# MLP biases as a broadcast second operand in two PSUM evacuations, with a new unit order

## The chip, the cores and the metric

One core of one Trainium2 chip. The time is the device time of one execution in microseconds (us); the kernel before takes 1090.31 us (median of 3 runs, 1090.11 to 1090.38). All runs quoted here are at a granted clock of 0.998 to 1.0. The same kernel spreads over more than that across rounds and chips: the kernel before had 9 runs from 1088.80 to 1092.16 us on one chip.

## The reference

An attention block whose output is gated by an MLP (S = 2048, D = 1024, 32 heads of 32, F = 3584):

```python
def _A_ref(x, wqkv, wo):                 # attention
    qkv = ...                            # x @ wqkv, split in heads
    scores = einsum("bhqd,bhkd->bhqk", q, k) * (Dh ** -0.5)
    o = einsum("bhqk,bhkd->bhqd", softmax(scores), v)
    return o.transpose(...) @ wo
def _B_ref(x, w1, b1, w2, b2):           # MLP
    h = gelu(layernorm(x) @ w1 + b1)     # tanh form of gelu
    return h @ w2 + b2
xn = layernorm(A_x)
return A_x + _A_ref(xn, ...) * silu(_B_ref(xn, ...))
```

## The kernel before

A planner in Python builds five instruction streams (one per engine) ahead of time. 512 attention units run one after the other; each takes one filler unit with it, in the order that the string PLAN gives: `a` = 1/28 of the first MLP matmul of a token chunk, `w2`..`w5` = one block of the second MLP matmul cut into 2 to 5 pieces, `q`, `v` = projections for the next heads, `o` = output projection, `.` = nothing. The loop, cut:

```python
while u < NU + LAG or ...:
    s_unit(u)                  # TensorE: scores, 32x128 tiles          (L872)
    fill_act(u)                # ScalarE: waiting tanh, if they fit     (L565, L609)
    exp_unit(u)                # ScalarE: two exponentials, 128x1024    (L884)
    ...                        # TensorE: one filler unit into bank 7   (L395)
    pv_unit(u - LAG)           # TensorE: P x V and row sums, 128x32    (L901, L904)
    run_dq(pg.clk["tensor"])   # VectorE: waiting gelu and softmax steps
```

The two evictions of the filler bank, and what follows the first of them (cut):

```python
x0 = op("vector", lambda e: e.tensor_scalar(xb[:, 0:n], bank(bk, 0, n), b1T[:, f:f + 1], None, op0=ALU.add),
   r=[("b", bk), "b1"], w=[kx], c=217 + 1.042 * n)                                   # L548
def square(): ... tensor_tensor(ub, xb, xb, mult)                                    # L554
def cube():   ... scalar_tensor_tensor(ub, ub, 1.0 / 0.044715, xb, add, mult)        # L558
def tanh():   ... activation(ut[:, :, 0:n], ut[:, :, 0:n], Tanh, scale=...)          # L565, ScalarE, two `a` at once
def gate():   ... scalar_tensor_tensor(hT, ut, 1.0, xq, add, mult)                   # L571
...
x0 = op("vector", lambda e: e.tensor_scalar(zh[:, 0:n], bank(bk, 0, n), 0.25, b2h[:, nb:nb + 1], op0=ALU.mult, op1=ALU.add),
   r=[("b", bk), "b2"], w=[kz], c=217 + 1.042 * n)                                   # L605
```

`c` is the planner's estimate of the duration in ns. It costs nothing on the chip, but the planner places the other VectorE and ScalarE operations by it. All filler units use bank 7, so the eviction of one filler has to be done before the next filler begins; in between lie the PV product and the next scores. `n` is 352 or 320 columns.

The softmax here doesn't subtract the row's maximum and nothing guards it: scores larger than these inputs give would overflow.

## Time and profile before

| | kernel before |
|---|---|
| time, us | 1090.31 |
| TensorE busy | 1078.1 us, 99% |
| ScalarE busy | 1043.9 us, 96% |
| VectorE busy | 627.6 us, 58% |
| L548, 352 / 320 columns | 584 / 551 ns |
| L605, 352 / 320 columns | 584 / 548 ns |
| score loads to filler loads | 0.33 us, with or without an eviction |

Two engines are nearly full and the third, which the change makes faster, is not. The lines behind this table are shown in the prediction, except the two of L605 (busy us, mean ns):

```profile
L605 DVE TENSOR_SCALAR zh<-ps,b2h 128x352 f32<-128x352 f32 x32 | 18.7, 584 | 141.6 <-PE ps L395 141.6
...
L605 DVE TENSOR_SCALAR zh<-ps,b2h 128x320 f32<-128x320 f32 x16 | 8.8, 548 | 41.8 <-PE ps L395 41.8
```

What is to be read from this profile is where TensorE can lose time at a unit boundary: in front of the scores, where it may wait for an exponential (L872 behind L884), and in front of the filler, where it may wait for the eviction (L395 behind L548 or L605).

### The profile page before, as it was taken

The page shows a single profiled execution, that of the slowest core. Times are in us where ns is not written, and L with a number is a line of the kernel's source. Part 1 is how long each engine was busy: PE and PEld are TensorE (multiplying, and loading weights), DVE is VectorE, ACT ScalarE, POOL GpSimd, SP SyncE. Part 2 cuts the span into 40 slices and gives each one's busy share as a digit, 9 for nine tenths or more (in the row PEclk, how much of TensorE's full clock was granted, in tenths as well). Part 3 has the DMA queues.
Part 4 walks back from the last instruction along what each step waited for, and adds up shares of the span by engine and source line. Part 5 has one row for each costly group of instructions (what it writes and reads, how often), then busy time and mean ns, then how long its engine had stood idle before and what let it go on. Part 6 is the DMA issues. An engine that isn't in the chain of part 4 may idle for free.

```text
span 1088.8 us, 61842 instructions
## 1 busy us (share of the span) xinstructions
PE 1078.1 (99%) x29167; PEld 701.4 (64%) x29167; DVE 627.6 (58%) x1396; ACT 1043.9 (96%) x1197; POOL 22.4 (2%) x69
## 2 busy tenths in 40 slices
PE   9999999999999999999999999999999999999998
PEld 6766666666666666666666666666666666666665
DVE  8487843477732576642377743378733387635556
ACT  7899998999999999999999999999999999999993
POOL 4400000000000000000000000000000000000000
PEclk9999999999999999999999999999999999999999
DMA  7944365413464214355333274423253343684534
GB/s 242 185 127 139 119 177 138 125 52 110 119 154 123 68 59 128 101 104 148 90 100 100 73 155 124 120 81 109 81 135 115 91 123 106 192 206 105 109 92 123
DMA packets 209336, 131.92 MB, mean 121 GB/s; under 512 B 52538, under 2 KB 200250, under 8 KB 209082
## 3 DMA queue, kind: packets, MB, share of 16 engines
q1 hardware_dynamic: 209082, 127.97, 43.4%
q8 instruction: 228, 3.74, 1.5%
q14 instruction: 26, 0.21, 0.1%
HBM read 104.87 MB, written 12.06 MB: 107 GB/s over the span
## 4 chain that ended last, share of the span: by engine, by line
PE 57%; ACT 41%; DVE 1%; DMA 0%; issue 0%; POOL 0%; SPq 0%
ACT P L884 37%; PE ps L395 34%; PE ps L872 9%; PE ps L901 6%; PE ps L904 6%; ACT u L565 4%; PE ps L705 1%; PE ps L689 1%; DVE stats L324 0%; DMA OT<-in_A_x_dram 0%; ACT thz L609 0%; DVE wq L669 0%; DVE hT L359 0%; ACT hT L716 0%; DVE wq L671 0%
## 5 line engine op out<-in xcount | busy, mean ns | idle before, releaser
L884 ACT ACTIVATE P<-ps 128x1024 bf16<-128x1024 f32 x1024 | 968.9, 1084 | 10.3 <-PE ps L872 5.4
L901 PE MATMUL ps<-P,VP 128*32 128x256 bf16 x4096 | 257.0, 273 | 0.5 <-issue 0.5
L904 PE MATMUL ps<-P,ones 128*32 128x256 bf16 x4096 | 256.8, 273 | 0.0
L395 PE MATMUL ps<-hT,war 128*32 128x352 bf16 (+1 forms) x5376 | 225.8, 309 | 0.1
L395 PE MATMUL ps<-yTc,war 128*32 128x352 bf16 (+1 forms) x5376 | 225.3, 309 | 0.0
L872 PE MATMUL ps<-QT,KT 32*128 32x256 bf16 x4096 | 203.7, 273 | 3.4 <-issue 0.6
L395 PEld LDWEIGHTS ps<-hT,war 128*32 128x32 bf16 x5376 | 128.0, 96 | 74.4 <-issue 25.8
L395 PEld LDWEIGHTS ps<-yTc,war 128*32 128x32 bf16 x5376 | 127.3, 96 | 74.2 <-DVE xb L548 18.9
L872 PEld LDWEIGHTS ps<-QT,KT 32*128 32x128 bf16 x4096 | 60.8, 92 | 115.6 <-issue 61.9
L605 DVE TENSOR_SCALAR zh<-ps,b2h 128x352 f32<-128x352 f32 (+1 forms) x48 | 27.5, 572 | 183.4 <-PE ps L395 183.4
L548 DVE TENSOR_SCALAR xb<-ps,b1T 128x352 f32<-128x352 f32 (+1 forms) x168 | 96.2, 573 | 48.7 <-PE ps L395 44.2
L571 DVE SCALAR_TENSOR_TENSOR hT<-u,xb 128x352 bf16<-128x352 f32 (+1 forms) x168 | 84.4, 509 | 68.3 <-ACT u L565 68.2
L901 PEld LDWEIGHTS ps<-P,VP 128*32 128x32 bf16 x4096 | 109.8, 97 | 21.3 <-issue 2.1
L904 PEld LDWEIGHTS ps<-P,ones 128*32 128x32 bf16 x4096 | 109.7, 97 | 18.6
L395 PE MATMUL ps<-xnT,wq 128*32 128x352 bf16 (+1 forms) x2688 | 112.7, 309 | 0.0
L395 PEld LDWEIGHTS ps<-xnT,wq 128*32 128x32 bf16 x2688 | 63.7, 96 | 37.2 <-DVE xb L548 8.9
L558 DVE SCALAR_TENSOR_TENSOR u<-u,xb 128x352 f32<-128x352 f32 (+1 forms) x168 | 82.5, 509 | 1.9
L554 DVE TENSOR_TENSOR u<-xb 128x352 f32<-128x352 f32 (+1 forms) x168 | 82.5, 507 | 0.7
L565 ACT ACTIVATE u<-u 128x704 f32<-128x704 f32 (+1 forms) x84 | 71.8, 859 | 0.0
L395 PE MATMUL ps<-xnT,OT 128*32 128x352 bf16 (+2 forms) x1568 | 62.9, 306 | 0.2 <-DVE wq L669 0.2
L395 PE MATMUL ps<-wq,xnT 128*32 128x256 bf16 x1536 | 50.8, 274 | 0.0
L395 PEld LDWEIGHTS ps<-xnT,OT 128*32 128x32 bf16 x1568 | 37.9, 96 | 19.7 <-DVE wq L669 7.7
(61 smaller groups left out, 477.3 us busy)
## 6 DMA issues: line engine op xcount, KB each, us to landing
war<-in_B_w_dram SPq DMA_DIRECT2D x336, 256.0 KB, 3.4
wq<-in_A_wqkv_dram SPq DMA_DIRECT2D x36, 128.0 KB, 2.3
OT<-in_A_x_dram SPq DMA_DIRECT2D x16, 256.0 KB, 5.7
xnT<-in_A_x_dram SPq DMA_DIRECT2D x16, 256.0 KB, 2.9
out_dram<-wq SPq DMA_DIRECT2D x15, 256.0 KB, 2.0
y_scratch<-OT SPq DMA_DIRECT2D x14, 256.0 KB, 2.4
gT_scratch<-gst SPq DMA_DIRECT2D x32, 88.0 KB, 3.3
xnT<-in_A_wo_dram SPq DMA_DIRECT2D x8, 256.0 KB, 4.0
```

The costliest lines, as they stand in the source:

```text
L395: ins = e.matmul(outs(j), lhsT=lhs(j), rhs=rhs, start=start, stop=stop, tile_position=(0, 32 * j), skip_group_check=True)
L548: x0 = op("vector", lambda e: e.tensor_scalar(xb[:, 0:n], bank(bk, 0, n), b1T[:, f:f + 1], None, op0=ALU.add), r=[("b", bk), "b1"], w=[kx] ...
L554: x = op("vector", lambda e: e.tensor_tensor(ub[:, 0:n], xb[:, 0:n], xb[:, 0:n], op=ALU.mult), r=[kx], w=[ku], c=151 + 1.042 * n)
L558: x = op("vector", lambda e: e.scalar_tensor_tensor(ub[:, 0:n], ub[:, 0:n], 1.0 / 0.044715, xb[:, 0:n], op0=ALU.add, op1=ALU.mult), r=[kx, ...
L565: x = op("scalar", lambda e: e.activation(ut[:, :, 0:n], ut[:, :, 0:n], ACT.Tanh, scale=0.7978845608028654 * 0.044715), r=kus, w=kus, c=48 ...
L571: op("vector", lambda e: e.scalar_tensor_tensor(hT[:, fq, 0:n], ut[:, i, 0:n], 1.0, xq[:, 0:n], op0=ALU.add, op1=ALU.mult), r=[kus[i], kq] ...
L605: x0 = op("vector", lambda e: e.tensor_scalar(zh[:, 0:n], bank(bk, 0, n), 0.25, b2h[:, nb:nb + 1], op0=ALU.mult, op1=ALU.add), r=[("b", bk ...
L689: ins = e.matmul(bank(bk, off, off + w), lhsT=wq[:, which, dc, 0:128], rhs=xnT[:, dc, t0 + lo:t0 + lo + w], start=dc == 0, stop=dc == DC - ...
L872: ins = e.matmul(bank(bks[j], kh * 256, (kh + 1) * 256), lhsT=KT[i2][32 * j:32 * j + 32, k0:k0 + 128], rhs=QT[i2][32 * j:32 * j + 32, qb * ...
L884: op("scalar", lambda e, p=p, sl=sl: e.activation(pb[:, 2 * p:2 * p + 2, :, :].rearrange("p a b q -> p (a b q)"), ps[:, sl * 1024:(sl + 1) ...
L901: e.matmul(bankq(ACC, j, 0, QW), lhsT=VP[vp][:, kb, vo + 32 * j:vo + 32 * j + 32], rhs=pb[:, j, kh, :], start=first, stop=False, tile_posi ...
L904: ins = e.matmul(bankq(ACC, j, QW, 2 * QW), lhsT=ones[:, 0:32], rhs=pb[:, j, kh, :], start=False, stop=last, tile_position=(0, 32 * j), sk ...
```

## The change

The intent: an eviction whose bias is a per-partition scalar takes some 60 ns longer than one whose second operand is a tensor. So the bias is given as a tensor that repeats along the row. The planner's estimate goes down by 52 ns, and the unit order was searched again for it.

```diff
-q a a a a q a a q a q v a a a q q a a v v a a a v v a a a a a a a q v a a q v ... (order before, cut)
+q a a a q a a q a a q v a a a q q a a v v a a a v v a a v a a a a q a a a q v ... (order after, cut)
-x0 = op("vector", lambda e: e.tensor_scalar(xb[:, 0:n], bank(bk, 0, n), b1T[:, f:f + 1], None, op0=ALU.add),
-   r=[("b", bk), "b1"], w=[kx], c=217 + 1.042 * n)
+x0 = op("vector", lambda e: e.tensor_tensor(xb[:, 0:n], bank(bk, 0, n), b1T[:, f:f + 1].to_broadcast((128, n)), op=ALU.add),
+   r=[("b", bk), "b1"], w=[kx], c=165 + 1.042 * n)
-x0 = op("vector", lambda e: e.tensor_scalar(zh[:, 0:n], bank(bk, 0, n), 0.25, b2h[:, nb:nb + 1], op0=ALU.mult, op1=ALU.add),
-   r=[("b", bk), "b2"], w=[kz], c=217 + 1.042 * n)
+x0 = op("vector", lambda e: e.scalar_tensor_tensor(zh[:, 0:n], bank(bk, 0, n), 0.25, b2h[:, nb:nb + 1].to_broadcast((128, n)), op0=ALU.mult, op1=ALU.add),
+   r=[("b", bk), "b2"], w=[kz], c=165 + 1.042 * n)
```

The two orders hold the same units; 50 of 518 slots differ (a `w` cut into k pieces counts as k slots).

## The prediction

> **What bounds the kernel now.** I read the page first (busy times and the chain that ended last), then the list of waits of the weight-load engine and ScalarE, then a few microseconds of the timeline on each side of a unit boundary, and last the VectorE groups with the shapes kept apart.
>
> ```profile
> PE 1078.1 (99%) x29167; PEld 701.4 (64%) x29167; DVE 627.6 (58%) x1396; ACT 1043.9 (96%) x1197; POOL 22.4 (2%) x69
> ...
> PE 57%; ACT 41%; DVE 1%; DMA 0%; issue 0%; POOL 0%; SPq 0%
> ```
>
> TensorE and ScalarE share the bound, 57% and 41% of the chain; VectorE has 1% of it, although it is busy for 58% of the span. The main part of the kernel is 512 attention units. In each, TensorE does scores (L872), one filler unit in bank 7 (L395: `a` = a block of the first MLP matmul, `w` = a piece of the second, `q` and `v` = projections, `o` = the output projection), then the PV product (L901, L904), while ScalarE does two exponentials. The two edited instructions, L548 and L605, empty bank 7 after `a` and after the last piece of a `w`. The question is therefore whether TensorE waits for them. The list of waits seems to say that it does:
>
> ```profile
> PEld ps L872 <- issue: 61.9, 290, 0.8
> PEld ps L872 <- ACT P L884: 53.3, 220, 0.5
> PEld ps L395 <- DVE xb L548: 34.3, 162, 0.3
> PEld ps L395 <- issue: 30.8, 145, 0.4
> PEld ps L395 <- DVE zh L605: 10.1, 48, 0.2
> ...
> PEld ps L395 <- DVE VP L435: 7.4, 35, 0.2
> ```
>
> Columns: total us, times, longest. 34.3 us behind L548 and 10.1 behind L605 look like a prize of 44 us. But divide: 34.3/162 = 0.212 us, 10.1/48 = 0.210, behind the much shorter VP cast 7.4/35 = 0.211, and behind nothing at all ("issue") 30.8/145 = 0.212. A wait that is the same for an eviction of 584 ns, one of 423 ns and none is not a wait for the eviction. The timeline shows it:
>
> ```profile
> 400.02 0.55 DVE L548 TENSOR_SCALAR xb<-ps,b1T 128x320 f32<-128x320 f32 x1
> ...
> 400.33 0.12 PEld L872 LDWEIGHTS ps<-QT,KT 32*128 32x128 bf16 x8 [0.21 <-issue]
> ...
> 400.66 0.94 PEld L395 LDWEIGHTS ps<-yTc,war 128*32 128x32 bf16 x32 [0.21 <-DVE xb L548]
> ...
> 491.71 0.12 PEld L872 LDWEIGHTS ps<-QT,KT 32*128 32x128 bf16 x8 [0.21 <-issue]
> ...
> 492.04 0.80 PEld L395 LDWEIGHTS ps<-hT,war 128*32 128x32 bf16 x28 [0.21 <-issue]
> ```
>
> From the score loads to the filler loads it is 400.66 - 400.33 = 0.33 us with an eviction in between, and 492.04 - 491.71 = 0.33 us between two pieces of one `w`, where nothing is evicted. I checked all 505 such places in the trace: 502 have 0.32 to 0.33 us, 119 of them with no eviction pending; the three exceptions sum to 0.23 us. The eviction (ending at 400.02 + 0.55 = 400.57) lands a hair before TensorE could go on anyway. What TensorE really loses is before the scores, where the base is 0.21 too: 53.3 - 220 x 0.21 = 7.1 us (6.8 us when I add up the single gaps), the exponential of an earlier unit not yet done. All of it is in stretches full of `a`, where ScalarE also has the gelu tanh (L565). Inside the filler units the stalls sum to 0.4 us.
>
> **What the Trainium skill says.** "VectorE: DVE Perf Modes", section The perf-mode tier table, gives `tensor_tensor` with any PSUM operand one element per cycle, and the section Why PSUM operands drop a tier gives fp32 from PSUM the same for any operation. So the slope cannot change, only the fixed part. The trace agrees: from 320 to 352 columns the old form grows by 584 - 551 = 33 ns and the PSUM `tensor_tensor` L669 by 524 - 491 = 33 ns, 1.03 ns per column. The same page's section on the errata states (N+151)/0.96 ns for an fp32 `tensor_tensor`: 524 ns at 352 columns. Measured are 518 from SBUF (L554) and 524 from PSUM (L669): it agrees. "DVE: scalar operands, raw-bit mode, write accounting and state across instructions", section 1, says that a pointer scalar does not take up the second tensor stream. It states no fixed cost for it; the 60 ns below are from the trace. "TensorEngine Tiling (Array Packing)", section Key Properties, says that changing the tiling mode drains the TensorE. The scores use 32x128 tiles, everything else 128x32, and the 0.21 us appear at each change of the two: it agrees.
>
> **The change part by part.**
>
> ```profile
> L548 DVE TENSOR_SCALAR xb<-ps,b1T 128x352 f32<-128x352 f32 x112 | 65.4, 584 | 31.5 <-PE ps L395 28.0
> L571 DVE SCALAR_TENSOR_TENSOR hT<-u,xb 128x352 bf16<-128x352 f32 x112 | 57.7, 520 | 43.6 <-ACT u L565 43.6
> ...
> L548 DVE TENSOR_SCALAR xb<-ps,b1T 128x320 f32<-128x320 f32 x56 | 30.8, 551 | 17.2 <-PE ps L395 16.2
> L924 DVE STREAM_TRANSPOSE trs<-r8s 128x256 f32<-128x256 f32 x64 | 28.3, 442 | 1.5
> L917 DVE STREAM_TRANSPOSE trs<-ps 128x256 f32<-128x256 f32 x64 | 28.2, 440 | 0.0
> ...
> L669 DVE TENSOR_TENSOR wq<-ps,xnT 128x352 f32<-128x352 f32 x32 | 16.8, 524 | 19.4 <-PE ps L395 19.3
> ```
>
> Part 1, L548. It becomes a `tensor_tensor` from PSUM with the bias repeated along the row. The nearest row is L669: 524 ns at 352 columns (491 at 320). A repeated operand should cost nothing: L924 reads a repeated source in 442 ns, L917 an ordinary one in 440. So 112 x (584 - 524) + 56 x (551 - 491) = 6.7 + 3.4 = 10.1 us of VectorE. Part 2, L605. It becomes a `scalar_tensor_tensor`, in this kernel 520 ns from SBUF (L571), so about 525 from PSUM: 32 x (584 - 525) + 16 x (548 - 492) = 1.9 + 0.9 = 2.8 us. VectorE falls by 12.9 us in all, to about 615 us. On the path TensorE can take from this only the three exceptional places, at most 0.2 us. ScalarE waits for L605 nine times (6.6 us), and 9 x 0.06 = 0.5 us of that goes, but the matmuls bound those places.
>
> Part 3, the order. The two orders have the same 168 `a`, 84 `q`, 48 `v`, 48 `w` and 49 `o`; 50 of 518 slots differ, nearly all in four `a` stretches (slots 4-48, 151-176, 250-275, 333-338). So no work is added or removed; only TensorE's waits for ScalarE can shrink. In those four stretches I count 0.9 + 1.3 + 0.9 + 0.3 = 3.4 us of them, counting each to the end of its `a` run. How much of that depends on the order? ScalarE takes 0.917 us per exponential (8 in 7.33 us in the chain), so 1.83 per unit, and a tanh for two `a` adds 0.67 (0.61 in 320-column chunks), so 2.17 per `a` unit. TensorE takes 2.07 for an `a` or `q` at 352 columns, 1.97 at 320, 1.75 for a `v` (unit periods in the trace). ScalarE's surplus is +0.10 per `a` (+0.17 at 320 columns), +0.08 per `v`, about -0.22 per `q`. In the first stretch, 28 x 0.10 + 8 x 0.08 - 12 x 0.22 = +0.8 us against 0.9 of measured waits; in the third, 21 x 0.10 + 7 x 0.08 - 7 x 0.22 = +1.1 against 0.9. The waits are about the whole surplus of a stretch, and a permutation inside it leaves that sum alone. What is left is to carry a backlog better into the `w` pieces that follow: I put it at 0.1 to 0.2 us per stretch, an estimate, in sum 0.5 us. This is a choice.
>
> Sum: 1090.31 - 0.1 (evictions) - 0.5 (order) = 1089.7 us.
>
> **Rivals.** (1) The evictions do bound TensorE: if the 44 us were real, 216 x 0.06 = 13 us would come off (1077 us). Against it: the equal 0.21 us with no eviction. (2) VectorE is the bound in runs of `a`: four operations there cost 584 + 518 + 519 + 520 = 2.14 us, about 1.8 when the 0.08 us overlap between neighbours is taken off, plus the accumulator chain, in units of 2.07 us; then earlier cubes give earlier tanh and smoother ScalarE, and most of the 3.4 us might go (1087 us). For it: the retuned order. Against it: L565 never waits in ScalarE's list. (3) The broadcast form is slower than thought, say 1.5 times: then 0.26 us more per eviction, 56 us at worst if all of it is exposed. Against it: L924. (4) The order, tuned on estimated times, fits the chip worse: some new waits of 0.1 to 0.2 us, +1 us (1091.3).
>
> **Range and chances.** The largest gain that the waits allow is 6.8 + 0.2 + 0.4 us, under 0.7%, and 2% would be 21.8 us. So only rival 3 leaves the band. Range 1088.2 to 1091.2 us, 8 in 10: down to half of rival 2, up to rival 4. Faster by over 2%: 0.005; within: 0.985; slower: 0.01.
>
> **What would show it.** L548 at 520 to 530 ns and L605 near 525, VectorE at 615 us; the wait of L395 behind L548 still 0.21 us each; TensorE's waits behind L884 still 6 to 8 us over the base, and TensorE's busy time the same within 1 us. I would be wrong if the 0.33 us between score and filler loads became shorter after evictions (rival 1), if those waits fell by 3 us or more (rival 2), or if the new forms took over 584 ns.

## The result, and the profile after

The changed kernel takes 1090.07 us (median of 6 runs, 1089.08 to 1091.40), the kernel before in the same rounds 1090.21 us (6 runs, 1088.63 to 1091.65). The ratio is 1.0002 with a 95% interval of 0.9989 to 1.0015: the same. (A ratio here is the mean time of one kernel's runs over that of the other's runs of the same rounds, so not quite the ratio of the medians.)

The page of the kernel after, busy times and chain:

```profile
PE 1077.6 (99%) x29167; PEld 701.1 (64%) x29167; DVE 614.1 (56%) x1396; ACT 1044.2 (96%) x1197; POOL 22.4 (2%) x69
...
PE 60%; ACT 38%; SPq 1%; DMA 1%; DVE 0%; issue 0%
```

VectorE lost 13.5 us, TensorE and ScalarE did not change. The list of waits of the kernel after (total us, times, longest):

```profile
PEld ps L872 <- issue: 63.0, 298, 0.2
PEld ps L872 <- ACT P L884: 51.7, 210, 0.6
PEld ps L395 <- DVE xb L548: 34.2, 162, 0.2
PEld ps L395 <- issue: 32.1, 152, 0.2
PEld ps L395 <- DVE zh L605: 9.9, 47, 0.2
```

The wait that is put down to L548 is 34.2/162 = 0.211 us, as before, although the eviction is 60 ns shorter. The VectorE groups of the kernel after, shapes kept apart (busy us, mean ns):

```profile
L548 DVE TENSOR_TENSOR xb<-ps,b1T 128x352 f32<-128x352 f32 x112 | 58.7, 524 | 36.0 <-PE ps L395 31.9
...
L548 DVE TENSOR_TENSOR xb<-ps,b1T 128x320 f32<-128x320 f32 x56 | 27.5, 491 | 17.8 <-PE ps L395 16.3
...
L605 DVE SCALAR_TENSOR_TENSOR zh<-ps,b2h 128x352 f32<-128x352 f32 x32 | 16.8, 524 | 143.9 <-PE ps L395 143.9
...
L605 DVE SCALAR_TENSOR_TENSOR zh<-ps,b2h 128x320 f32<-128x320 f32 x16 | 7.8, 487 | 41.3 <-PE ps L395 41.3
```

And the timeline of the kernel after at one boundary with an eviction (start us, duration us):

```profile
402.67 0.49 DVE L548 TENSOR_TENSOR xb<-ps,b1T 128x320 f32<-128x320 f32 x1
...
402.98 0.12 PEld L872 LDWEIGHTS ps<-QT,KT 32*128 32x128 bf16 x8 [0.21 <-issue]
...
403.31 0.94 PEld L395 LDWEIGHTS ps<-xnT,wq 128*32 128x32 bf16 x32 [0.21 <-DVE xb L548]
```

Score loads to filler loads is still 403.31 - 402.98 = 0.33 us. What did change is how long before the filler's first matmul the eviction ends: here 403.31 - (402.67 + 0.49) = 0.15 us, in the prediction's place, also with 320 columns, 400.66 - 400.57 = 0.09. Over all 168 evictions of L548 the median of this slack is 61 ns in the kernel before (smallest 56) and 121 ns in the kernel after; for L605 it goes from 59 to 120. So the whole 60 ns went into slack. These medians mix two shapes. L548 and L605 together, the slack goes from 59 to 119 ns at 352 columns (144 evictions) and from 92 to 152 ns at 320 (72 evictions).

One thing in the trace of before belongs to no wait of the kernel's: two long gaps inside a group of matmuls, one of them here, with no releaser but "issue":

```profile
542.24 0.10 PEld L872 LDWEIGHTS ps<-QT,KT 32*128 32x128 bf16 x3 [0.21 <-ACT P L884]
...
543.14 0.11 PEld L872 LDWEIGHTS ps<-QT,KT 32*128 32x128 bf16 x5 [0.81 <-issue]
```

This one is 0.79 us from matmul to matmul over the normal step, the other (in a PV product at 361.71) 0.68 us. The trace of the changed kernel has 0.11 us at a place near the latter and nothing near the former. From the start of unit 7 to that of unit 511 the kernel before took 1024.05 us and the changed one 1023.07; without those 1.47 us the changed kernel is 0.5 us longer, not shorter. As much as that is in its waits for ScalarE before the scores, which went from 6.8 to 7.3 us (next section).

### The profile page after: what moved, and what is told of

Read it like the earlier page. It is cut to its first block, busy times and chain, and to the rows that moved or that the text cites. A ratio compares the mean times of both kernels' runs of the same rounds, so it can differ in the third digit from the quotient of the medians.

```text
span 1088.3 us, 61842 instructions
## 1 busy us (share of the span) xinstructions
PE 1077.6 (99%) x29167; PEld 701.1 (64%) x29167; DVE 614.1 (56%) x1396; ACT 1044.2 (96%) x1197; POOL 22.4 (2%) x69
## 4 chain that ended last, share of the span: by engine, by line
PE 60%; ACT 38%; SPq 1%; DMA 1%; DVE 0%; issue 0%
PE ps L395 36%; ACT P L884 35%; PE ps L872 10%; PE ps L901 6%; PE ps L904 6%; ACT u L565 3%; PE ps L705 1%; PE ps L689 1%; DMA wq<-in_A_wqkv_dram 1%; SPq L275 0%; ACT thz L609 0%; DVE wq L669 0%; DVE wq L671 0%; PE ps L386 0%; SPq L285 0%
## 5 line engine op out<-in xcount | busy, mean ns | idle before, releaser
L605 DVE SCALAR_TENSOR_TENSOR zh<-ps,b2h 128x352 f32<-128x352 f32 (+1 forms) x48 | 24.6, 512 | 185.2 <-PE ps L395 185.2
L571 DVE SCALAR_TENSOR_TENSOR hT<-u,xb 128x352 bf16<-128x352 f32 (+1 forms) x168 | 84.5, 509 | 71.5 <-ACT u L565 71.5
L548 DVE TENSOR_TENSOR xb<-ps,b1T 128x352 f32<-128x352 f32 (+1 forms) x168 | 86.2, 513 | 53.9 <-PE ps L395 48.2
```

The source lines that it names most:

```text
L548: x0 = op("vector", lambda e: e.tensor_tensor(xb[:, 0:n], bank(bk, 0, n), b1T[:, f:f + 1].to_broadcast((128, n)), op=ALU.add), r=[("b", bk ...
L571: op("vector", lambda e: e.scalar_tensor_tensor(hT[:, fq, 0:n], ut[:, i, 0:n], 1.0, xq[:, 0:n], op0=ALU.add, op1=ALU.mult), r=[kus[i], kq] ...
L605: x0 = op("vector", lambda e: e.scalar_tensor_tensor(zh[:, 0:n], bank(bk, 0, n), 0.25, b2h[:, nb:nb + 1].to_broadcast((128, n)), op0=ALU.m ...
```

## The experiments

Twelve experiments ran, two of them repeats, in three calls; each call shares its runs of the kernel before. The table sums up what the traces hold. "Before fillers" is the time by which the step from the last score matmul to the first filler matmul exceeds its usual 197 ns, summed over all units; "before scores" is the same for the step from the PV product to the scores (usual 205 ns), that is, the waits for ScalarE; "inside fillers" sums the steps between rounds of a filler that are over 30 ns too long.

| kernel | median us | ratio to before, 95% interval | VectorE us | slack L548 ns | before fillers us | before scores us | inside fillers us |
|---|---|---|---|---|---|---|---|
| before | 1090.1 to 1090.3 | 1 | 627.6 | 61 | 0.5 | 6.8 | 0.3 |
| changed | 1090.07 | 1.0002 (0.9989-1.0015) | 614.1 | 121 | 0.4 | 7.3 | 0.3 |
| forms_only | 1088.85 | 0.9989 (0.9977-1.0002) | 615.3 | 121 | 0.4 | 6.7 | 0.1 |
| forms_again | 1089.15 | 0.9993 (0.9980-1.0005) | 615.7 | 120 | 0.4 | 6.9 | 0.0 |
| after_again | 1090.86 | 1.0005 (0.9993-1.0018) | 614.6 | 120 | 0.4 | 7.3 | 0.3 |
| order_only | 1090.33 | 1.0001 (0.9987-1.0014) | 625.6 | 60 | 0.6 | 7.2 | 0.2 |
| before_plus64 | 1096.19 | 1.0056 (1.0042-1.0069) | 641.9 | 55 | 11.6 | 2.3 | 0.3 |
| after_plus64 | 1089.66 | 0.9998 (0.9984-1.0012) | 627.1 | 55 | 1.0 | 6.8 | 0.1 |
| after_plus96 | 1093.29 | 1.0028 (1.0014-1.0042) | 634.7 | 55 | 6.7 | 4.3 | 0.4 |
| light_vector | 1090.32 | 1.0002 (0.9986-1.0017) | 562.6 | 119 | 0.4 | 7.3 | 1.2 |
| best_order | 1089.87 | 1.0000 (0.9988-1.0013) | 617.9 | 119 | 0.6 | 2.8 | 4.3 |
| after_cal | 1090.60 | 1.0008 (0.9994-1.0021) | 615.3 | 119 | 0.5 | 7.5 | 0.1 |
| half_tanh | 1084.01 | 0.9943 (0.9929-0.9956) | 614.4 | 119 | 0.3 | 0.5 | 0.1 |
| sorted_order | 1100.27 | 1.0097 (1.0081-1.0112) | 614.2 | 120 | 6.6 | 7.4 | 4.1 |

The theory: the eviction is hidden behind the PV product, the scores and the change of tiling mode; the 60 ns only add slack; and the waits for ScalarE are a surplus of ScalarE's work in the `a` stretches, which the new order hardly changes. The rivals: (A) the evictions bind TensorE, (B) VectorE's load in runs of `a` delays the tanh and so ScalarE, (C) one half of the change gains and the other half takes it back. (The expectations quoted below number their rivals each for itself.)

### The forms alone, and the order alone

forms_only is the kernel before with the two new instructions and nothing else; order_only is the changed kernel with the two old ones put back. `c` stays as the kernel at hand has it, so the order of instructions on every engine is exactly that of the kernel it was made from.

```diff
 # forms_only: kernel before, c unchanged
-e.tensor_scalar(xb[:, 0:n], bank(bk, 0, n), b1T[:, f:f + 1], None, op0=ALU.add)
+e.tensor_tensor(xb[:, 0:n], bank(bk, 0, n), b1T[:, f:f + 1].to_broadcast((128, n)), op=ALU.add)
-e.tensor_scalar(zh[:, 0:n], bank(bk, 0, n), 0.25, b2h[:, nb:nb + 1], op0=ALU.mult, op1=ALU.add)
+e.scalar_tensor_tensor(zh[:, 0:n], bank(bk, 0, n), 0.25, b2h[:, nb:nb + 1].to_broadcast((128, n)), op0=ALU.mult, op1=ALU.add)
 # order_only: changed kernel, the same four lines the other way round
```

> The kernel before with the two eviction forms exchanged and nothing else: same unit order, same order of instructions on every engine. Theory (the eviction is hidden behind the mode change, it only gains slack): VectorE busy 614 us instead of 627.6, slack from the end of an eviction to the next filler load about 120 ns instead of 60, the 0.33 us from score loads to filler loads unchanged, TensorE's waits for ScalarE unchanged at 7 us over the base; ratio to the kernel before 0.9990 to 1.0010. Rival 1 (evictions bound TensorE): 5 to 13 us faster, ratio 0.988 to 0.995. Rival 2 (the new order spoiled a gain of the forms): 1 to 3 us faster than the kernel before, and faster than the changed kernel by as much.

> The changed kernel with the two old eviction forms put back and nothing else, so the new unit order and its instruction order with evictions 60 ns longer than that order was made for. Theory: slack falls back to about 60 ns in the median, a few late evictions now bind (up to 0.5 us in all), otherwise the same: ratio to the kernel before 0.9990 to 1.0012. Rival 1 (evictions bound TensorE): same as before as well, so this run alone does not tell; Rival 2 (the order is the part that costs): 0.5 to 2 us slower than the kernel before and the changed kernel no slower only thanks to the forms.

The ratio of order_only, 1.0001, lies in what the theory expected; that of forms_only, 0.9989, just outside it (0.9990). The slack of forms_only is 121 ns and its waits for ScalarE are 6.7 us against 6.8, both as the theory had it, and the 5 to 13 us of rival A are excluded. But forms_only has the lowest time of the call, 1088.85 us, which speaks for rival C. So both were repeated on one chip, with five rounds each. forms_again is the same kernel as forms_only, after_again the same as the changed one; there is no edit.

> The forms alone once more (order of the kernel before). The last call gave a ratio of 0.9989 with an interval of 0.9977 to 1.0002, which does not settle whether the forms alone gain 1 us. If the gain is real: ratio 0.9985 to 0.9995 and 0.5 to 1.5 us under the changed kernel. If it was chance: both within 0.4 us of each other.

> The changed kernel itself once more, on the same chip as the forms alone. Theory: the same as the kernel before, ratio 0.9990 to 1.0010. If the new order costs (the forms alone were 1.2 us under the kernel before in the last call, the order alone 0.3 above): 0.5 to 1.5 us slower than the forms alone in this call.

The forms alone again come out under the changed kernel: mean 1089.40 us of five runs (1088.52 to 1090.62) against 1090.77 (1089.62 to 1091.96), 1.4 us. The traces agree with each other: from unit 7 to unit 511 the two traces of the forms alone take 1021.95 and 1021.81 us, the two of the changed kernel 1023.07 and 1023.02. Of these 1.2 us, 0.4 to 0.6 are longer waits before the scores (7.3 us against 6.7 and 6.9). These waits repeat from trace to trace. In units 150 to 185 and 250 to 285, where most of the changed slots lie, they are 0.41 and 0.72 us in the three traces with the old order, and 0.66 to 0.67 and 1.13 us in the three with the new one, order_only among them. In units 0 to 55 it is the other way: 0.86 to 0.87 us with the old order, 0.63 to 0.72 with the new. The clearest single one is where the new order has five `a` and then four `v` in a row, in the changed kernel:

```profile
574.06 0.12 PEld L872 LDWEIGHTS ps<-QT,KT 32*128 32x128 bf16 x8 [0.60 <-ACT P L884]
```

Here the wait is 0.60 us instead of 0.21. All of those nine units have ScalarE in surplus, so its backlog has nothing to shrink in. So the new order costs 0.4 to 0.6 us of waits for ScalarE, shown by the traces, and about 1.2 us in all under the new instructions, of which the rest is not assigned. Under the old instructions no cost of the order shows in the times: order_only has the ratio 1.0001, with an interval of 0.9987 to 1.0014. Whether the forms alone beat the kernel before stays open: 0.9989 and 0.9993 both lie in what forms_again expected of a real gain (0.9985 to 0.9995), but both intervals include 1.

### Longer evictions: where is the edge?

If the slack is all that the change gained, a longer eviction has to cost the kernel before at once, and the changed kernel only beyond its slack. I let both evictions read and write more columns of bank 7 than are used (the results stay right); the tiles are made wider by as much.

```diff
 # before_plus64; after_plus64 and after_plus96 likewise on the changed kernel, with 64 and 96
-xb_t = [sb(f"xb{i}", [128, CW], F32) for i in range(NXB)]
+xb_t = [sb(f"xb{i}", [128, CW + 64], F32) for i in range(NXB)]
-e.tensor_scalar(xb[:, 0:n], bank(bk, 0, n), b1T[:, f:f + 1], None, op0=ALU.add)
+e.tensor_scalar(xb[:, 0:n + 64], bank(bk, 0, n + 64), b1T[:, f:f + 1], None, op0=ALU.add)
 # zh_t and the eviction of w in the same way
```

> The kernel before with both evictions reading and writing 64 more columns of bank 7 than are used (results stay right): about 67 ns longer each, 651 ns at 352 columns. Theory: the kernel before has 57 to 61 ns between the end of an eviction and the next filler load, and the smallest of all such gaps, where TensorE does wait, is 55 ns; so it stands 2 to 6 ns from the edge, and 67 ns more make TensorE wait some 61 ns after most of the 216 evictions, 13 us less what the 7 us of waits for ScalarE absorb: 5 to 11 us slower (ratio 1.005 to 1.010), the score-to-filler time 0.39 us instead of 0.33. Rival (the eviction has real room before it): under 1 us slower.

> The changed kernel with the same 64 idle columns added to both evictions: 591 ns at 352 columns. Theory: slack 121 - 67 = 54 to 55 ns, just at the edge, so 0 to 1 us slower than the changed kernel (ratio to the kernel before 0.9990 to 1.0015), where the kernel before pays 5 to 11 us for the same addition. Rival (a longer eviction costs in both alike because VectorE's time is what counts): slower by the same amount as the kernel before with 64 columns.

> The changed kernel with 96 idle columns in both evictions, about 100 ns longer each. Theory: slack 121 - 100 = 21 ns, 34 ns under the 55 ns of the edge, so the score-to-filler time grows to 0.36 us; 216 x 34 ns = 7.3 us, of which the waits for ScalarE absorb about half (with 64 columns the kernel before paid 11.2 us more there and got 5.0 back): 3 to 5 us slower than the changed kernel, where 64 columns cost it nothing. Rival (no edge, cost in proportion to VectorE's time): 64 columns cost 0, so 96 cost 0 to 1 us.

Waits of the kernel before with 64 columns more:

```profile
PEld ps L872 <- ACT P L884: 41.1, 184, 0.4
...
PEld ps L395 <- DVE zh L605: 12.6, 48, 0.3
```

and of the changed kernel with 64 columns more:

```profile
PEld ps L872 <- ACT P L884: 52.3, 215, 0.6
...
PEld ps L395 <- DVE zh L605: 10.2, 48, 0.2
```

The wait behind L605 is 12.6/48 = 0.263 us in the first and 10.2/48 = 0.213 us in the second. The first two came out as expected: +6 us (ratio 1.0056) and nothing (0.9998). The third costs 3 us against the kernel before (1.0028), but 2.5 us against the changed kernel (means 1093.28 and 1090.77), a little under the 3 to 5 us expected. In each of the three the median slack sits at 55 ns, and no trace has less than 54: that is how long after the end of an eviction TensorE can start when it does wait for it. The kernel before stood 59 - 55 = 4 ns from that edge at 352 columns and 92 - 55 = 37 ns at 320; the changed one stands 64 and 97 ns from it. This accounts for the cost: 67 ns more should make TensorE wait 144 x (67 - 4) + 72 x (67 - 37) ns = 11.2 us, and before_plus64 waits 11.6 - 0.5 = 11.1 us more before the fillers. And a wait of TensorE is not always a loss: before_plus64 gets 4.5 us back before the scores (2.3 us against 6.8; the expectation of after_plus96 says 5.0), because a TensorE that comes later finds the exponential done.

### Is it VectorE or ScalarE that holds TensorE in the `a` stretches?

```diff
 # light_vector: changed kernel, the square over 32 columns only; wrong on purpose
-e.tensor_tensor(ub[:, 0:n], xb[:, 0:n], xb[:, 0:n], op=ALU.mult)
+e.tensor_tensor(ub[:, 0:32], xb[:, 0:32], xb[:, 0:32], op=ALU.mult)
-e.scalar_tensor_tensor(ub[:, 0:n], ub[:, 0:n], 1.0 / 0.044715, xb[:, 0:n], op0=ALU.add, op1=ALU.mult)
+e.scalar_tensor_tensor(ub[:, 0:n], xb[:, 0:n], 1.0 / 0.044715, xb[:, 0:n], op0=ALU.add, op1=ALU.mult)
 # half_tanh: changed kernel, tanh over half the columns; wrong on purpose
-e.activation(ut[:, :, 0:n], ut[:, :, 0:n], ACT.Tanh, ...)
+e.activation(ut[:, :, 0:n // 2], ut[:, :, 0:n // 2], ACT.Tanh, ...)
```

> The changed kernel with the square of the gelu chain shrunk to 32 columns (the result is wrong on purpose: the cube then reads x where it should read x squared). Same instructions, same order, VectorE some 168 x 0.32 = 54 us lighter, all of it in the a stretches. Theory (ScalarE, not VectorE, holds TensorE there): time within 0.7 us, TensorE's waits for ScalarE still 6 to 8 us over the base. Rival 2 of the prediction (VectorE bounds the runs of a): those waits fall by 2 us or more and so does the time.

> The changed kernel with the gelu tanh run over half its columns (wrong result on purpose), same instructions and order: ScalarE saves about 0.28 us per tanh, 24 us in all, and its time per a unit falls from 2.17 to about 2.02 us, under TensorE's 2.07. Theory (ScalarE's surplus in the a stretches is the one thing that holds TensorE): the waits fall from 7.3 to under 1.5 us and the time by 5 to 7 us (ratio 0.994 to 0.9955). Rival (something else takes their place, VectorE or the evictions): under 3 us.

One line of the waits of light_vector, then the same of half_tanh:

```profile
PEld ps L872 <- ACT P L884: 51.7, 210, 0.6
```

```profile
PEld ps L872 <- ACT P L884: 26.1, 121, 0.4
```

With 51.5 us less work on VectorE the line is the same as in the changed kernel to the last digit, and the time too (1090.32 us). With less work on ScalarE it falls to 26.1/121 = 0.216 us each, the base; the waits before the scores go from 7.3 to 0.5 us and the time falls by 6 us (0.9943). Rival B falls; ScalarE's surplus is what is left for TensorE to wait for. (half_tanh is wrong by a relative error of 0.022; light_vector, although its gelu is wrong, stayed within the tolerance.)

### What can the order do?

sorted_order takes the first stretch of the changed kernel and sorts it.

```diff
-q a a a q a a q a a q v a a a q q a a v v a a a v v a a v a a a a q a a a q v q a a a q a q q w2 v ...
+a a a a a a a a a a a a a a a a a a a a a a a a a a a a q q q q q q q q q q q q v v v v v v v w2 v ...
```

> The changed kernel with its first stretch (slots 0 to 46) sorted: 28 a, then 12 q, then 7 v. The same work in the stretch, so the same sum of surpluses, but nothing evens it out. Ledger: 28 x 0.10 = 2.8 us of waits for ScalarE less some 0.3 us of backlog, against 0.8 us now: 1.5 to 2.5 us slower. Rival: in a pure run of a VectorE is full as well (523 + 518 + 518 + 520 ns less 4 x 84 of overlap = 1.74 us, with accumulators and normalisation about 2.15 us per unit of 2.17), evictions come late and the time rises by 4 to 8 us, with score-to-filler times over 0.33 us.

It costs 10 us, which is more than either side expected, and not in the waits before the scores (7.4 us). The timeline of sorted_order shows two new kinds of wait:

```profile
60.54 0.14 PEld L395 LDWEIGHTS ps<-yTc,war 128*32 128x32 bf16 x8 [2.72 <-DMA war<-in_B_w_dram]
...
112.54 0.53 DVE L571 SCALAR_TENSOR_TENSOR hT<-u,xb 128x352 bf16<-128x352 f32 x1 [0.86 <-ACT u L565]
113.17 0.53 DVE L548 TENSOR_TENSOR xb<-ps,b1T 128x352 f32<-128x352 f32 x1
113.75 0.27 PEld L395 LDWEIGHTS ps<-yTc,war 128*32 128x32 bf16 x12 [2.83 <-DVE xb L548]
```

With the `a` close together, MLP weights were asked for before they had landed (3.2 of the 4.1 us inside fillers). After the longer of these waits the trace shows a granted TensorE clock of 0.50 for 3.4 us (60.6 to 64.0 us), and a round of a filler took 0.29 us there instead of 0.15; that is another 0.7 us of the 4.1. And an eviction stood in VectorE's queue behind a gate (L571) that waited for its tanh, so bank 7 came free late: two places of 2.0 and 2.6 us make up most of the 6.6 us before fillers. A third of 1.2 us, the first filler of all, waited for the DMA of its input (yTc). The ledger of ScalarE's surplus is right only while weights, inputs and gates come in time.

best_order is the attempt to use what the experiments point to. The planner prices an exponential at 903 ns and a tanh at 634 ns (352 columns), where the chain in the trace shows 916 and 667. I put the measured costs in and searched the order again; the search moved `q`, where TensorE is in surplus, into the `a` stretches, and `v` out of them. after_cal has the corrected costs alone.

```diff
 # after_cal and best_order
-... ACT.Exp, scale=SCALE), ... c=903.0)
+... ACT.Exp, scale=SCALE), ... c=916.5)
-act_tasks.append((x.t + 60.0, tanh, 48 + 1.666 * n, cur["u"]))        # and the same cost in the tanh itself
+act_tasks.append((x.t + 60.0, tanh, 80 + 1.666 * n, cur["u"]))
 # best_order only
-q a a a q a a q a a q v a a a q q a a v v a a a v v a a v a a a a q ...
+a a a q a a a a v q a a a a q q a q v v q a a a v a a q q a q q a q v v v ...
```

> The changed kernel with (1) the kernel's own planning costs of ScalarE set to what the traces show (916.5 ns per exponential instead of 903, tanh 666 ns at 352 columns instead of 634) and (2) a unit order searched with them. Between the first and last a of the six chunks it has 76 q and 29 v where the changed kernel has 67 and 41: q and v change places with the w stretches. Ledger of the prediction: 9 x 0.22 + 12 x 0.08 = 3.0 us less surplus of ScalarE, so TensorE's waits for ScalarE fall from 7.3 to about 4 us and the time by 2 to 4 us (ratio to the kernel before 0.996 to 0.998). Rival (order can't gain, waits only move, or new waits for late q, v or gates take the place): within 1 us of the kernel before.

> Control for best_order: the changed kernel with only the two planning costs corrected (they place tanh and VectorE operations differently among the others), the unit order of the changed kernel kept. Theory: the gain of best_order is its order; this one stays within 0.7 us of the changed kernel. Rival: the placement of the tanh is what gains, then this one shows most of it.

The waits for ScalarE fell even further than the ledger said, from 7.3 to 2.8 us, and after_cal (7.5 us) shows that the order did it. But the time did not move (1089.87 us, ratio 1.0000), where 2 to 4 us were expected: the rival side was right. Waits of best_order, and its longest new one in the timeline:

```profile
PEld ps L872 <- ACT P L884: 48.1, 215, 0.4
...
PEld ps L395 <- DMA war<-in_B_w_dram: 3.9, 6, 1.2
```

```profile
438.84 0.12 PEld L395 LDWEIGHTS ps<-yTc,war 128*32 128x32 bf16 x8 [1.18 <-DMA war<-in_B_w_dram]
```

4.5 us came off before the scores and 4.0 us came on inside the fillers (4.3 against 0.3), most of it for MLP weights that were not there yet. So there was no version that beats both kernels by a clear margin; the forms with the old order have the lowest times of those that ran with right results.

## Why the prediction was right, step by step

- **The evictions are hidden (right).** Predicted: the wait of 0.21 us stays and TensorE gains 0.1 us. It stayed at 0.211, and before the fillers the sum went from 0.46 to 0.36 us. That the wait put down to L548 is no wait for L548 is shown by forms_only, where it stays although the eviction is 60 ns shorter, and by before_plus64 and after_plus64: the same 64 columns cost 6 us where there was little slack and nothing where there was more. What I did not see is how near it was: I wrote that the eviction ends a hair early, from a place with 320 columns, where the hair was 37 ns; at 352 columns it was 4 ns.
- **The durations (right).** 524 and 491 ns for L548 as predicted from L669 (the 524 ns that the prediction works out from (N+151)/0.96 are an estimate from that page), 524 and 487 for L605 where I had 525 and 492; VectorE 614.1 us where I had 615.
- **The order (wrong in sign).** This term, 0.5 us of gain, is the step that failed. Under the new instructions the new order is 1.2 us longer in the traces and 1.4 us in the times; 0.4 to 0.6 us of that are waits for ScalarE, the rest is spread over small gaps that I can't assign. My ledger gave the sum of a stretch, said that a permutation leaves it alone, and I then guessed that a new search would use the backlog better. It did not: the waits went up from 6.8 to 7.3 us. Slots 151 to 176 and 250 to 275 hold the same units in both orders, and yet the waits there rose, from 0.41 to 0.67 and from 0.72 to 1.13 us; the second is where `a` and `v` were put side by side. The ledger was also rougher than it looks. By its own periods a `q` is 1.83 - 2.07 = -0.24 us, not -0.22, and the first stretch has 7 `v`, not 8, so that its surplus is 0.5 us and not 0.8, against 0.9 us measured.
- **The forms alone (perhaps more than 0.1 us).** Their two ratios point to 0.7 to 1.2 us of gain. The traces show 0.1 us before the fillers and no less waiting for ScalarE (6.7 and 6.9 us against 6.8). From unit 7 to unit 511 they are 2.1 and 2.2 us shorter than the one trace of before, but 1.47 us of that are its two gaps of "issue". This stays open.
- **The rivals (settled).** Rival 1 fell with forms_only, rival 2 with light_vector, rival 3 (a slow broadcast) with the durations. Rival 4, new waits of 1 us from the new order, is the one nearest to what happened. If the gain of the forms is real, the loss by the order cancels it. That the sum, 1089.7 us, lies within 0.4 us of the measured 1090.07 is then partly luck: a gain by the order was counted that did not come.

## What to carry to other kernels

Before a wait in a list is counted as a prize, divide it by its count and look for the same wait where its named cause is absent: 0.21 us behind every eviction and behind none goes with the change of tile shape, not with the eviction (from a filler to the PV product, where the shape stays, the load engine's median idle time is 0.04 us). Slack is a result too, and a median over two shapes hides it: at 352 columns the kernel before stood 4 ns from an edge behind which TensorE waits for a longer eviction, and an extra 67 ns cost it 6 us and the changed kernel nothing. When two engines are both almost full, waits that a new order takes from one place can come back in another (in best_order they went from ScalarE to the DMA of the MLP weights), so a new order has to be measured apart from the instructions it comes with.

## What the Trainium skill lacked or had wrong

- "VectorE: DVE Perf Modes", section on the errata: its table gives PSUM to SBUF as 120 + FD cycles, from which 492 ns at 352 columns are an estimate. Measured are 584 ns with a per-partition scalar and 524 ns with a tensor operand. The page's formula for an fp32 `tensor_tensor`, (N+151)/0.96, fits the latter to the nanosecond, from PSUM too, which the page does not say.
- "DVE: scalar operands, raw-bit mode, write accounting and state across instructions", section 1: it has no time for reading a pointer scalar. In this kernel the form with one takes 60 ns longer than the form with a repeated tensor (584 against 524, 551 against 491; the opcode changes with it, and no run separates the two), and the repeated operand itself costs nothing (524 ns with the bias repeated, 524 with an ordinary tensor).
- "TensorEngine Tiling (Array Packing)", section Key Properties: it says that a mode change drains TensorE but not for how long. Here the load engine sits idle for 0.21 us at each change between 32x128 and 128x32 tiles, twice per unit.
- I found on none of the pages how soon TensorE starts after a VectorE instruction that it waits for: 55 ns from the end of the eviction to the first matmul, in 197 of the 216 evictions of after_plus96, to within 1 ns.
